# Scores ahead of everything in TensorE's written-out order, denominators inverted on one row per head, and more exponentials on VectorE

## The chip, the cores and the metric

One core of one Trainium2 chip. Time is device time in microseconds (us); the kernel before has a median of 2510.38 us over three runs (2509.66 to 2510.57). TensorE (PE) multiplies matrices, with weight loads beside it (PEld); VectorE (DVE), ScalarE (ACT) and GpSimd (POOL) work elementwise; SyncE (SP) issues the DMA transfers.

## The reference

Two layers, and each is a linear attention with a softmax feature map (A) followed by an ordinary softmax attention (B), both behind a layer norm and with a residual. Sequence 2048, width 1024, 32 heads of 32, bfloat16.

```python
def _A_ref(x, wqkv, w_phi, wo):          # q, k, v: 32 heads of 32
    pq = jnp.einsum("bhsd,hdf->bhsf", q, w_phi)
    pk = jnp.einsum("bhsd,hdf->bhsf", k, w_phi)
    phi_q = jnp.concatenate([_softmax(pq, axis=-1), _softmax(-pq, axis=-1)], axis=-1)
    phi_k = jnp.concatenate([_softmax(pk, axis=-1), _softmax(-pk, axis=-1)], axis=-1)
    kv = jnp.einsum("bhsf,bhsd->bhfd", phi_k, v)
    z  = jnp.einsum("bhsf->bhf", phi_k)
    num = jnp.einsum("bhqf,bhfd->bhqd", phi_q, kv)
    den = jnp.einsum("bhqf,bhf->bhq", phi_q, z)[..., None] + 1e-6
    o = num / den                        # then transposed, times wo

def _B_ref(x, wqkv, wo):
    scores = jnp.einsum("bhqd,bhkd->bhqk", q, k) * (Dh ** -0.5)
    p = _softmax(scores, axis=-1)
    o = jnp.einsum("bhqk,bhkd->bhqd", p, v)   # then transposed, times wo

for _ in range(2):
    x = x + _A_ref(_layernorm(x, axis=-1), A_wqkv, A_w_phi, A_wo)
    x = x + _B_ref(_layernorm(x, axis=-1), B_wqkv, B_wo)
```

## The kernel before

**How the program comes about.** The kernel doesn't issue instructions as it goes. It describes every piece of work as an `Op` with an engine, an assumed duration, dependencies, buffers and a priority (a due time; lower is earlier), and `Sched.run` plays these through a small model of the chip. The order in which the model starts the pieces is the order in which the instructions are written to each engine's queue; on the chip each engine then works through its queue in order. On each engine the model takes the ready piece with the lowest priority whose buffers can be had; it looks past at most 60 that can't start, and at nothing more than `WINDOW` = 80 ahead of the earliest piece not yet started. Buffers have quotas by class (`QUOTA`): SBUF pieces come from one large tile called `arena`, so nearly everything in the profile is called `arena`; PSUM has eight banks. A wait that the chip needs because a piece of arena is used again follows from where the model put it.

**The stages.** The sequence is cut into four chunks of 512 tokens, the heads into eight groups of four (`g`). Attention A is done chunk by chunk. Attention B has 32 turns a layer: a turn is one chunk of queries (`qc`) and one group of heads. The first 16 turns go over the groups for chunks 0 and 1, the rest over the groups for chunk 2 and then 3. A turn has two halves (`pp`), each with eight blocks of keys times four heads, so 64 units of 128 keys by 512 queries.

**Scores and exponentials.** Three units make a group. Their three matmuls (line 1006, each on 32 of TensorE's rows, beside one another) fill three banks of PSUM, banks 0 to 2 and 3 to 5 in turn; one ScalarE instruction (line 1012) takes the exponential of all 1536 columns into a tile of class `E`, of which there are five. The product with the values (line 1042) adds up in bank 6, with the sums of the exponentials (a matmul with ones) beside it: per half, two heads' outputs on 64 partitions and their denominators on the other 64, each denominator repeated on 32 partitions. A copy (line 1057, tile class `T`) empties bank 6 on VectorE. The priorities are the turn's due time less 2 for scores, less 3 for exponentials, less 1 for the products and less 4 for the copy.

**The filling.** Bank 7 belongs to everything else that TensorE does meanwhile: projections of the next heads' keys, queries and values, the output projection of finished chunks, and in the first layer the next layer's attention A on chunks 0 to 2, all through the helper at line 425 with priorities of their own. Where the model finds TensorE idle for a good part of 3.4 us, it writes idle matmuls (line 1253, with a weight of zeros).

**Units on VectorE.** `exp_dve` computes the exponential of two units at a time with ten VectorE instructions (lines 949 to 966) from bank 7. `EXTRA` says in which turns of which layer, and how many; these units are left out of ScalarE's groups.

**Denominators.** After the second half of a turn two transfers (lines 1083 and 1085, 128 KB each, on SP) bring both halves' denominators into one tile (`den`), four reciprocals of 128 columns (line 1087) invert it, and two products (line 1091) give the turn's output (`oT`), which the output projection reads later. The last turn of a layer goes another way, without transfers (lines 1067 to 1078).

Of the kernel before, what the change touches and what calls it, by code (L numbers as in the profile page):

```python
# [11 lines left out]
ALU = mybir.AluOpType  # L12
AX = mybir.AxisListType
BF16 = mybir.dt.bfloat16
F32 = mybir.dt.float32
# [5 lines left out]
C512 = 512  # L21
# [11 lines left out]


class Op:
    __slots__ = ("eng", "dur", "lat", "fn", "bufs", "prio", "mode", "ndep", "out", "t", "start", "seq", "accum")

    def __init__(self, eng, dur, lat, fn, bufs, prio, mode, seq):
        self.eng, self.dur, self.lat, self.fn, self.bufs = eng, dur, lat, fn, bufs
        self.prio, self.mode, self.seq = prio, mode, seq  # L40
        self.ndep, self.out, self.t, self.start, self.accum = 0, [], 0.0, None, None


LAT = {"PE": 0.25, "ACT": 0.2, "DVE": 0.1, "POOL": 0.2, "SP": 2.0, "AQ": 2.0}
# [3 lines left out]
class Sched:  # L48
# [11 lines left out]
    def op(self, eng, dur, fn, deps=(), bufs=(), prio=0.0, lat=None, mode=None):  # L60
        o = Op(eng, dur, LAT[eng] if lat is None else lat, fn, tuple(bufs), prio, mode, len(self.ops))
        for d in deps:
            if d is not None:
                d.out.append(o)
                o.ndep += 1
        for b in o.bufs:
            b.left += 1
        self.ops.append(o)
        return o
# [75 lines left out]
    def run(self):  # L145
        engines = list(LAT)
# [19 lines left out]
        started = {}  # L166
        for o in self.ops:
            if o.ndep == 0:
                heapq.heappush(ready[o.eng], (o.prio, o.seq, o))
        t, left, order = 0.0, len(self.ops), []  # L170
        while left:
            moved = False
            for e in engines:
                if busy[e] > t + 1e-9 or not ready[e]:
                    continue
                skipped = []
                pick = None
                while ready[e] and len(skipped) < 60:
                    item = heapq.heappop(ready[e])
                    if item[0] <= todo[front] + WINDOW and self._alloc(item[2].bufs):  # L180
                        pick = item[2]
                        break
                    skipped.append(item)
                for s in skipped:
                    heapq.heappush(ready[e], s)
                if pick is None and e == "PE" and self.idle is not None and self.live.get("S", 0):

                    recent = [r for r in recent if r[1] > t - SPELL]
                    worked = sum(r[1] - max(r[0], t - SPELL) for r in recent)
                    if worked >= KEEP * SPELL:  # L190
                        pass
                    elif self.bank_used[7]:

                        if accum:
                            pick = Op("PE", MM, LAT["PE"], self.idle_acc, (), 0.0, "c", 0)
                            left += 1
                    elif not self.live.get("fil", 0):
                        pick = Op("PE", MM, LAT["PE"], self.idle, (Buf("ps", 0, "idle", [(7,)]),), 0.0, "c", 0)
                        pick.bufs[0].left = 1
                        self.queue["idle"] = [list(pick.bufs), 0]  # L200
                        assert self._alloc(pick.bufs)
                        left += 1
                if pick is None:
                    continue
                if e == "PE":
                    recent.append((t, t + pick.dur))
                    if pick.accum is not None:
                        accum = pick.accum
                d = pick.dur
                if pick.mode is not None:  # L210
                    if mode[e] is not None and mode[e] != pick.mode:
                        d += SWITCH
                    mode[e] = pick.mode
                pick.start = t
                if pick.fn not in (self.idle, self.idle_acc):
                    started[pick.prio] = started.get(pick.prio, 0) + 1
                while front < len(todo) - 1 and started.get(todo[front], 0):
                    started[todo[front]] -= 1
                    front += 1
                busy[e] = t + d  # L220
                order.append(pick)
                left -= 1
                moved = True
                n += 1
                heapq.heappush(events, (t + d, n, pick, True))
                n += 1
                heapq.heappush(events, (t + d + pick.lat, n, pick, False))
            if moved:
                continue
            if not events:  # L230
                stuck = [(o.prio, o.eng, [(b.cls, b.at) for b in o.bufs]) for e in engines for _, _, o in ready[e]][:8]
                raise AssertionError(f"nothing can start at {t:.1f}: {left} left, {stuck}, live {self.live}")
            t = events[0][0]
            while events and events[0][0] <= t + 1e-9:
                _, _, o, own = heapq.heappop(events)
                if not own:
                    for b in o.bufs:
                        b.left -= 1
                        if b.left == 0:
                            self._release(b)  # L240
                for x in o.out:

                    if own != (x.eng == o.eng and x.eng not in ("SP", "AQ")):
                        continue
                    x.ndep -= 1
                    if x.ndep == 0:
                        heapq.heappush(ready[x.eng], (x.prio, x.seq, x))
        self.end = t
        return order

# [4 lines left out]
LONG = {"kT", "v", "slab", "slabk", "xn", "xn1", "kvacc", "kvm", "zm", "wnat"}  # L255
MODEST = {"slabk", "xn1", "e1", "vp1", "pkf", "lnw1", "w2o"}
QUOTA = {"pk": 3, "pv": 2, "kv": 1, "ln": 2, "mm": 2, "cmp": 2, "bc": 4, "num": 1, "wt": 4, "fil": 2,
# [4 lines left out]
SPELL = 3.4  # L262
KEEP = 0.75
# [3 lines left out]
POW2_0 = 0.998010015430466  # L267
POW2_C = (-2.753493604392706, 3.611980637904819, -2.738565741928622)
LEAD = 5.0
EXTRA = (lambda i: [(i % 2, 2)] if 12 <= i < 17 else [],  # L270
         lambda i: [(0, 2), (1, 2)] if 16 < i < 30 and i % 4 else [(i % 2, 2)] if 8 <= i < 30 else [])


def act_us(n):
    return n / 1200 + 0.064


def dve_us(n):
    return n / 960 + 0.15
# [6 lines left out]
def kernel(  # L286
# [15 lines left out]
    G = PO  # L302
# [67 lines left out]
    wdq_v = wd_q[:].rearrange("(po pi) f -> pi po f", pi=P)  # L370
    wdk_v = wd_k[:].rearrange("(po pi) f -> pi po f", pi=P)

    qd = dram_p.tile([P, 2 * G * C512], BF16, tag="qd")
    qd_v = qd[:].rearrange("p (c g n) -> p c g n", c=2, g=G)
    xd = dram_p.tile([P, 3 * PO * C512], BF16, tag="xd")
# [39 lines left out]
    def dma(prio, fn, deps=(), bufs=(), q="SP", kb=256, issue=0.55):  # L415
        return op(q, issue, fn, deps, bufs, prio, lat=2.0 + kb / 200.0)
# [554 lines left out]
    def attention(base, kT, vT, q_of, gate, extra):  # L971
# [16 lines left out]
        while i < len(units):  # L988
# [14 lines left out]
            def sfn(grp=grp, s_v=s_v):  # L1003
                for x, (qc, g, pp, d, j) in enumerate(grp):
# [4 lines left out]
                        rhs=q_of[(qc, g)][1]()[r, (pp + j // 2) % 2, :],  # L1009
                        start=True, stop=True, tile_position=(32 * j, 0))  # L1010
            so = op("PE", 0.24, sfn, deps + (gate if n == 0 else []), [s_b, *bufs], prio - 2, mode="r")
            ex = op("ACT", act_us(w * C512), lambda s_v=s_v, e_v=e_v, w=w: nc.scalar.activation(  # L1012
                out=e_v()[:, 0:w * C512], in_=s_v(), func=ACT.Exp, scale=4 * math.log(2)),
                [so], [s_b, e_b], prio - 3)
# [6 lines left out]
        if True:  # L1021
            for qc, g in turns:
# [41 lines left out]
                if end:  # L1064
# [15 lines left out]
                        [ln], [o_b, l_b, a_b], prio))  # L1080
                    oTs[qc][g] = (o_b, o_v, s)
                    continue
                m1 = dma(prio, lambda d_v=d_v, T=T: nc.sync.dma_start(out=d_v()[hi_, :], in_=T[0][1]()[hi_, :]),
                         [T[0][2]], [d_b, T[0][0]], kb=128)
                m2 = dma(prio, lambda d_v=d_v, T=T: nc.sync.dma_start(out=d_v()[lo_, :], in_=T[1][1]()[lo_, :]),
                         [T[1][2]], [d_b, T[1][0]], kb=128)
                rc = [op("DVE", 128 * 8 / 960 + 0.12, lambda b=b, d_v=d_v, r_v=r_v: nc.vector.reciprocal(  # L1087
                    out=r_v()[:, b * P:(b + 1) * P], in_=d_v()[:, b * P:(b + 1) * P]), [m1, m2], [d_b], prio)
                    for b in range(4)]
                o_b, o_v = sb("oT", C512)  # L1090
                s = [op("DVE", dve_us(512), lambda a=a, b=b, k=k, o_v=o_v, r_v=r_v, T=T: nc.vector.tensor_tensor(
                    out=o_v()[a, :], in0=T[k][1]()[a, :], in1=r_v()[b, :], op=ALU.mult),
                    rc, [o_b, r_b, T[k][0]], prio)
                    for k, (a, b) in enumerate(((lo_, hi_), (hi_, lo_)))]
                oTs[qc][g] = (o_b, o_v, s)
        return oTs, so

# [191 lines left out]
```

## Time and profile before

| | |
|---|---|
| median of three runs | 2510.38 us |
| the profiled execution | 2511.27 us, its span 2509.5 us |
| mean granted TensorE clock | 0.994 |
| exponentials (line 1012) of the first layer | first starts at 357.6 us, last ends at 1343.8 us |
| of the second layer | 1566.4 to 2497.5 us |
| their busy time | 1812.4 us in 1342 instructions |
| VectorE units | 37 of two blocks (lines 949 to 966), 9.0 us each |
| reciprocals (line 1087) | 248, 212.9 us busy |

The span runs from the first to the last instruction of the program. Busy times of an engine are shares of that span; instructions of one engine can overlap by some hundred ns, so the distance between two starts is shorter than the duration in a row.

### The profile page before, as it was taken

How to read it: one execution, taken by the hardware profiler on the slowest of the kernel's cores; microseconds unless marked ns; L12 is line 12 of the kernel's file. 1: busy time of each engine (PE TensorE's matmuls, PEld its weight loads, DVE VectorE, ACT ScalarE, POOL GpSimd, SP SyncE). 2: the span in 40 equal slices, each digit the busy share in tenths (PEclk: the TensorE clock that was granted, in tenths of full speed). 3: DMA queues.
4: the chain of work that ended last, by engine and by line, in shares of the span. 5: the costliest groups of instructions: out<-in, count | busy, mean ns of one | idle time of the engine just before them, and what ended most of it. 6: DMA issues, size and time to landing. Idle time of an engine off the chain costs nothing.

```text
span 2509.5 us, 62924 instructions
## 1 busy us (share of the span) xinstructions
PE 2368.6 (94%) x27872; PEld 893.4 (36%) x27872; DVE 1468.5 (59%) x2003; ACT 2145.4 (85%) x1897; POOL 26.1 (1%) x72
## 2 busy tenths in 40 slices
PE   7999999999999999999999999999999999999998
PEld 4443433333333333333333444333333333333333
DVE  6997653333356345654646766333356578687854
ACT  6335558999999999999996465699999999999998
POOL 0000000000000000000000000000000000000000
PEclk9999999999999999999999999999999999999999
DMA  9110012111121222222323001111121100110000
GB/s 219 33 44 1 22 21 48 35 36 44 41 62 42 56 54 69 77 66 69 114 65 116 1 5 38 36 36 35 40 62 27 35 27 27 29 33 27 25 25 27
DMA packets 185282, 117.39 MB, mean 47 GB/s; under 512 B 103344, under 2 KB 175024, under 8 KB 184240
## 3 DMA queue, kind: packets, MB, share of 16 engines
q1 hardware_dynamic: 183952, 111.26, 16.7%
q8 instruction: 218, 3.57, 0.6%
q10 hardware_dynamic: 1056, 2.10, 0.3%
q14 instruction: 56, 0.46, 0.1%
HBM read 62.46 MB, written 15.73 MB: 31 GB/s over the span
## 4 chain that ended last, share of the span: by engine, by line
ACT 46%; PE 31%; issue 12%; DVE 8%; SPq 1%; DMA 1%; ACTq 0%; DVEq 0%
ACT arena L1012 43%; PE psum L421 14%; PE psum L425 5%; PE psum L1042 5%; PE psum L1006 4%; DVE arena L616 1%; SPq L456 1%; PE psum L1253 1%; PE psum L780 1%; ACT arena L612 1%; DVE arena L625 1%; DVE arena L963 1%; DVE arena L662 1%; DVE arena L510 1%; DVE arena L514 1%
## 5 line engine op out<-in xcount | busy, mean ns | idle before, releaser
L1012 ACT ACTIVATE arena<-psum 128x1536 bf16<-128x1536 f32 x1342 | 1812.4, 1566 | 50.5 <-PE psum L1006 43.7
L1042 PE MATMUL psum<-arena 128*32 128x512 bf16 x4096 | 699.0, 385 | 11.6 <-ACT arena L1012 8.4
L1042 PE MATMUL psum<-arena,ones_bf 128*32 128x512 bf16 x4096 | 700.3, 386 | 0.0
L1006 PE MATMUL psum<-arena 32*128 32x512 bf16 x4022 | 522.8, 383 | 74.6 <-ACT arena L1012 68.3
L425 PE MATMUL psum<-arena 128*32 128x512 bf16 x8256 | 576.3, 380 | 4.9 <-DVE arena L625 1.3
L421 PE MATMUL psum<-arena 128*128 128x512 bf16 x2032 | 474.2, 383 | 18.1 <-DVE arena L514 5.4
L1006 PEld LDWEIGHTS <-arena 32*128 32x128 bf16 x4022 | 163.4, 91 | 574.8 <-issue 564.9
L421 PEld LDWEIGHTS <-arena 128*128 128x128 bf16 x2032 | 193.6, 98 | 265.8 <-issue 47.6
L425 PEld LDWEIGHTS <-arena 128*32 128x32 bf16 x8256 | 212.3, 96 | 209.8 <-issue 53.9
L1042 PEld LDWEIGHTS <-arena 128*32 128x32 bf16 x4096 | 165.8, 94 | 271.6 <-issue 246.5
L1087 DVE RECIPROCAL arena<-arena 128x128 f32<-128x128 f32 x248 | 212.9, 913 | 44.7 <-DMA arena<-arena 44.4
L1253 PE MATMUL psum<-xT,zero 128*32 128x512 bf16 x2712 | 218.5, 382 | 0.0
L839 DVE CAST arena<-psum 128x512 bf16<-128x512 f32 x112 | 77.3, 690 | 238.5 <-PE psum L425 238.1
L1042 PEld LDWEIGHTS <-ones_bf 128*32 128x32 bf16 x4096 | 158.4, 94 | 62.7 <-issue 50.8
L1057 DVE COPY arena<-psum 128x512 f32<-128x512 f32 x126 | 86.8, 689 | 157.3 <-PE psum L1042 155.6
L963 DVE SCALAR_TENSOR_TENSOR arena<-arena 128x1024 f32<-128x1024 f32 x111 | 135.6, 1222 | 2.3
L612 ACT ACTIVATE arena<-psum 128x512 bf16<-128x512 f32 x80 | 42.8, 600 | 86.1 <-PE psum L421 57.8
L742 ACT ACTIVATE arena<-psum 128x512 bf16<-128x512 f32 x128 | 69.8, 597 | 41.5 <-PE psum L421 32.0
L625 DVE TENSOR_TENSOR arena<-psum,arena 128x1024 bf16<-128x1024 f32 x64 | 78.3, 1224 | 39.6 <-PE psum L425 35.5
L510 DVE TENSOR_TENSOR arena<-xT,arena 128x1024 f32<-128x1024 bf16 x64 | 77.9, 1219 | 35.2 <-ACT arena L499 34.8
L1253 PEld LDWEIGHTS <-zero 128*32 128x32 bf16 x2712 | 70.3, 97 | 64.5 <-issue 16.8
L514 DVE TENSOR_TENSOR arena<-arena 128x1024 bf16<-128x1024 f32 x64 | 77.4, 1223 | 23.9 <-ACT arena L504 22.6
(100 smaller groups left out, 1428.3 us busy)
## 6 DMA issues: line engine op xcount, KB each, us to landing
arena<-arena SPq DMA_DIRECT2D x124, 128.0 KB, 2.2
arena<-in_A_wqkv_dram SPq DMA_DIRECT2D x10, 1024.0 KB, 5.5
arena<-in_B_wqkv_dram SPq DMA_DIRECT2D x32, 256.0 KB, 3.1
arena<-arena SPq DMA_DIRECT2D x256, 32.0 KB, 1.9
arena<-in_B_wo_dram SPq DMA_DIRECT2D x32, 256.0 KB, 3.0
arena<-wd_k SPq DMA_DIRECT2D x8, 1024.0 KB, 5.7
arena<-in_A_wo_dram SPq DMA_DIRECT2D x4, 1024.0 KB, 7.1
arena<-in_B_wqkv_dram SPq DMA_DIRECT2D x4, 1024.0 KB, 5.4
```

The lines of the kernel that those rows point to most:

```text
L421: nc.tensor.matmul(out_, lhsT=lhsT, rhs=rhs, start=start, stop=stop, skip_group_check=True)
L425: nc.tensor.matmul(out_[ks, :], lhsT=lhsT[:, ks], rhs=rhs, start=start, stop=stop, tile_position=(0, 32 * k), skip_group_check=True)
L510: s1 = op("DVE", dve_us(1024), lambda pr=pr, w_v=w_v: nc.vector.tensor_tensor(out=w_v(), in0=xT[:, pr, csl(c)], in1=m_v().unsqueeze(1).to_ ...
L514: fin.append(op("DVE", dve_us(1024), lambda pr=pr, w_v=w_v: nc.vector.tensor_tensor(out=xv()[:, pr, :], in0=w_v(), in1=r_v().unsqueeze(1). ...
L625: ml = op("DVE", dve_us(1024), lambda vpv=vpv, wv_=wv_, sv=sv: nc.vector.tensor_tensor(out=wv_()[:, :, :, 0:DH], in0=vpv().rearrange("p (h ...
L963: last = [op("DVE", dve_us(1024), lambda i=i, c=c: nc.vector.scalar_tensor_tensor(out=x_v(), in0=(x_v() if i else g_v()), scalar=c, in1=g_ ...
L1006: nc.tensor.matmul(out=s_v()[:, x * C512:(x + 1) * C512], lhsT=kT[g][1]()[r, pp, d * P:(d + 1) * P], rhs=q_of[(qc, g)][1]()[r, (pp + j // ...
L1012: ex = op("ACT", act_us(w * C512), lambda s_v=s_v, e_v=e_v, w=w: nc.scalar.activation(out=e_v()[:, 0:w * C512], in_=s_v(), func=ACT.Exp, s ...
L1042: nc.tensor.matmul(out=a_v()[col:col + 32, :], lhsT=v_v()[:, kc % 4, o:o + DH] if what == 0 else ones_bf[:], rhs=ev()[:, x * C512:(x + 1) ...
L1057: cp = op("DVE", dve_us(512), lambda t_v=t_v, a_v=a_v: nc.vector.tensor_copy(out=t_v(), in_=a_v()), [last], [a_b, t_b], prio - 4)
L1087: rc = [op("DVE", 128 * 8 / 960 + 0.12, lambda b=b, d_v=d_v, r_v=r_v: nc.vector.reciprocal(out=r_v()[:, b * P:(b + 1) * P], in_=d_v()[:, b ...
L1253: nc.tensor.matmul(psum[32 * k:32 * k + 32, 6 * C512:7 * C512], lhsT=zero[:], rhs=xT[:, 0, 0:C512], start=False, stop=False, tile_position ...
```

## The change

Three things change together.

Pieces of work get a flag `first`, set on all score groups from the third on; the model takes flagged pieces ahead of all others, whatever their priority. It looks past 400 pieces that can't start, not 60. There are six tiles of class `E`, not five.

Denominators are no longer inverted on 32 equal rows per head. Two transfers take one row per head (two from each half) and lay its 512 values out as 32 partitions of 16 (tile `cden`, 128 partitions by 16 columns). One reciprocal inverts them, a third transfer writes them to a tensor in HBM (`rd`), and a fourth reads them back with each row repeated on 32 partitions. The two products follow. The last turn's way is unchanged.

`EXTRA` gives VectorE two units (of two blocks) instead of one in turns 12 to 16 of the first layer; in the second, still one in turns 8 to 15, and in turns 16 to 29 two, or three in every third turn. In all 50 where there were 37, which is 26 blocks more.

```diff
-        self.ndep, self.out, self.t, self.start, self.accum = 0, [], 0.0, None, None
+        self.ndep, self.out, self.t, self.start, self.accum, self.first = 0, [], 0.0, None, None, False
...
-                heapq.heappush(ready[o.eng], (o.prio, o.seq, o))
+                heapq.heappush(ready[o.eng], (not o.first, o.prio, o.seq, o))
...
-                while ready[e] and len(skipped) < 60:
+                while ready[e] and len(skipped) < 400:
                     item = heapq.heappop(ready[e])
-                    if item[0] <= todo[front] + WINDOW and self._alloc(item[2].bufs):
-                        pick = item[2]
+                    if item[1] <= todo[front] + WINDOW and self._alloc(item[3].bufs):
+                        pick = item[3]
...
-                        heapq.heappush(ready[x.eng], (x.prio, x.seq, x))
+                        heapq.heappush(ready[x.eng], (not x.first, x.prio, x.seq, x))
...
-         "e": 6, "vp": 6, "e1": 4, "vp1": 4, "E": 5, "q2": 3, "kt": 3, "w2": 8, "w2o": 3, "oT": 26, "T": 4, "den": 2,
+         "e": 6, "vp": 6, "e1": 4, "vp1": 4, "E": 6, "q2": 3, "kt": 3, "w2": 8, "w2o": 3, "oT": 26, "T": 4, "den": 2,
...
-         "rs": 8, "pkf": 1, "part": 8, "w2r": 1,
+         "rs": 8, "pkf": 1, "cden": 2, "part": 8, "w2r": 1,
...
-EXTRA = (lambda i: [(i % 2, 2)] if 12 <= i < 17 else [],
-         lambda i: [(0, 2), (1, 2)] if 16 < i < 30 and i % 4 else [(i % 2, 2)] if 8 <= i < 30 else [])
+EXTRA = (lambda i: [(0, 2), (1, 2)] if 12 <= i < 17 else [],
+         lambda i: ([(0, 2), (1, 2)] if i % 3 else [(0, 2), (0, 5), (1, 4)]) if 16 <= i < 30 else [(i % 2, 2)] if 8 <= i < 16 else [])
...
+    rd = dram_p.tile([2 * NC * G * 4, C512], F32, tag="rd")
+    rd_v = rd[:].rearrange("(t h) n -> t h n", h=4)
+    gone = []
...
             so = op("PE", 0.24, sfn, deps + (gate if n == 0 else []), [s_b, *bufs], prio - 2, mode="r")
+
+            so.first = n >= 2
...
-                m1 = dma(prio, lambda d_v=d_v, T=T: nc.sync.dma_start(out=d_v()[hi_, :], in_=T[0][1]()[hi_, :]),
-                         [T[0][2]], [d_b, T[0][0]], kb=128)
-                m2 = dma(prio, lambda d_v=d_v, T=T: nc.sync.dma_start(out=d_v()[lo_, :], in_=T[1][1]()[lo_, :]),
-                         [T[1][2]], [d_b, T[1][0]], kb=128)
-                rc = [op("DVE", 128 * 8 / 960 + 0.12, lambda b=b, d_v=d_v, r_v=r_v: nc.vector.reciprocal(
-                    out=r_v()[:, b * P:(b + 1) * P], in_=d_v()[:, b * P:(b + 1) * P]), [m1, m2], [d_b], prio)
-                    for b in range(4)]
+                c_b, c_v = sb("cden", 16, dt=F32)
+                at_d = rd_v[len(gone)]
+                gone.append((qc, g))
+                m = [dma(prio, lambda k=k, c_v=c_v, T=T: nc.sync.dma_start(
+                    out=c_v()[64 * k:64 * k + 64, :],
+                    in_=T[k][1]()[64 * (1 - k):64 * (1 - k) + 64:32, :].rearrange("r (s c) -> r s c", c=16)),
+                    [T[k][2]], [c_b, T[k][0]], kb=4) for k in range(2)]
+                rc = op("DVE", 0.27, lambda c_v=c_v: nc.vector.reciprocal(out=c_v(), in_=c_v()), m, [c_b], prio)
+                aw = dma(prio, lambda c_v=c_v, at_d=at_d: nc.sync.dma_start(
+                    out=at_d.rearrange("h (s c) -> (h s) c", c=16), in_=c_v()), [rc], [c_b], kb=8)
+                bk = dma(prio, lambda r_v=r_v, at_d=at_d: nc.sync.dma_start(
+                    out=r_v(), in_=at_d.unsqueeze(1).to_broadcast([4, 32, C512])), [aw], [d_b], kb=256)
                 o_b, o_v = sb("oT", C512)
-                s = [op("DVE", dve_us(512), lambda a=a, b=b, k=k, o_v=o_v, r_v=r_v, T=T: nc.vector.tensor_tensor(
-                    out=o_v()[a, :], in0=T[k][1]()[a, :], in1=r_v()[b, :], op=ALU.mult),
-                    rc, [o_b, r_b, T[k][0]], prio)
-                    for k, (a, b) in enumerate(((lo_, hi_), (hi_, lo_)))]
+                s = [op("DVE", dve_us(512), lambda a=a, k=k, o_v=o_v, r_v=r_v, T=T: nc.vector.tensor_tensor(
+                    out=o_v()[a, :], in0=T[k][1]()[a, :], in1=r_v()[a, :], op=ALU.mult),
+                    [bk], [o_b, r_b, T[k][0]], prio)
+                    for k, a in enumerate((lo_, hi_))]
```

More of the change, by code (lines that the diff above doesn't have):

```diff
@@ L35 @@
 class Op:
-    __slots__ = ("eng", "dur", "lat", "fn", "bufs", "prio", "mode", "ndep", "out", "t", "start", "seq", "accum")
+    __slots__ = ("eng", "dur", "lat", "fn", "bufs", "prio", "mode", "ndep", "out", "t", "start", "seq", "accum", "first")
     def __init__(self, eng, dur, lat, fn, bufs, prio, mode, seq):
@@ L230, in run @@
             if not events:
-                stuck = [(o.prio, o.eng, [(b.cls, b.at) for b in o.bufs]) for e in engines for _, _, o in ready[e]][:8]
+                stuck = [(o.prio, o.eng, [(b.cls, b.at) for b in o.bufs]) for e in engines for _, _, _, o in ready[e]][:8]
                 raise AssertionError(f"nothing can start at {t:.1f}: {left} left, {stuck}, live {self.live}")
```

## The prediction

> **What bounds the kernel now.** I read the page first (busy time, the 40 slices, the costliest groups), then the windows, then ScalarE's and TensorE's rows in order of time, then the waits, last the transfers. In the slices the two attention stages are where ACT shows 9: slices 8 to 21 and 27 to 40.
>
> ```profile
> span 2509.5 us, 62924 instructions
> PE 2368.6 (94%) x27872; PEld 893.4 (36%) x27872; DVE 1468.5 (59%) x2003; ACT 2145.4 (85%) x1897; POOL 26.1 (1%) x72
> ...
> PE   7999999999999999999999999999999999999998
> ...
> DVE  6997653333356345654646766333356578687854
> ACT  6335558999999999999996465699999999999998
> ...
> L1012 ACT ACTIVATE arena<-psum 128x1536 bf16<-128x1536 f32 x1342 | 1812.4, 1566 | 50.5 <-PE psum L1006 43.7
> ...
> L1253 PE MATMUL psum<-xT,zero 128*32 128x512 bf16 x2712 | 218.5, 382 | 0.0
> ...
> L1087 DVE RECIPROCAL arena<-arena 128x128 f32<-128x128 f32 x248 | 212.9, 913 | 44.7 <-DMA arena<-arena 44.4
> ```
>
> TensorE's 94% is not a bound: L1253 is filling that multiplies zeros where nothing else is due. ScalarE in the windows is:
>
> ```profile
> 800.00:900.00 100.00, 96.09 (x1330) 33.17 (x1326) 38.70 (x50) 100.00 (x75) 0.00 (x0) 1.00 0.22 50
> 1000.00:1100.00 100.00, 92.47 (x1319) 36.67 (x1316) 63.19 (x92) 96.33 (x84) 2.90 (x8) 1.00 0.24 75
> 2300.00:2400.00 100.00, 91.66 (x1262) 31.24 (x1255) 85.27 (x103) 99.96 (x76) 0.00 (x0) 1.00 0.10 27
> ```
>
> Its cadence stands in its timeline: 44 exponentials in 59.36 us, less 1.57 for the last's own length: 1.34 us from start to start; over all neighbouring pairs the median is 1.331 us (a row's 1.566 us overlaps its neighbours). The first row is the longest wait at a stage's start.
>
> ```profile
> 368.44 1.45 ACT L1012 ACTIVATE arena<-psum 128x1536 bf16<-128x1536 f32 x1 [9.39 <-PE psum L1006]
> ...
> 1271.86 59.36 ACT L1012 ACTIVATE arena<-psum 128x1536 bf16<-128x1536 f32 x44
> ```
>
> The exponentials run from 357.6 to 1343.8 and from 1566.4 to 2497.5. Stage 1: 986.2 us = 680 x 1.331 (905.1) + 37.8 of other ScalarE work + 43.3 lost. Stage 2: 931.1 = 662 x 1.331 (881.1) + 8.6 + 41.4. About half of each loss (21.5 and 21.2) lies before the 26th exponential, where the last token chunk's keys are still being made; some 7 in each are slips of tens of ns. The rest, about 15 and 13, are waits, most of them for scores (L1006) that stand behind other TensorE work:
>
> ```profile
> PE psum L1006 <- ACT arena L1012: 68.3, 229, 3.7
> ...
> DVE arena L1087 <- DMA arena<-arena: 44.4, 28, 3.5
> ACT arena L1012 <- PE psum L1006: 43.7, 34, 9.4
> ```
>
> TensorE's prices, by starts in its timeline: from the scores' start to the next kind's 0.32 us, from the start of two groups of four column-tiled matmuls (x8) to the scores 0.55. So a group of four, or of three scores, is 0.21 us, and a turn between the kinds 0.11.
>
> ```profile
> 396.32 0.61 PE L425 MATMUL psum<-arena 128*32 128x512 bf16 x8
> 396.87 0.39 PE L1006 MATMUL psum<-arena 32*128 32x512 bf16 x3
> 397.19 1.48 PE L425 MATMUL psum<-arena 128*32 128x512 bf16 x24
> ```
>
> **The change part by part.** The sum is made against the profiled execution's own 2511.27 us (span 2509.5 and 1.8 around it), 0.9 above the median 2510.38.
>
> *More VectorE units.* A unit takes two 512-wide blocks off ScalarE. Units go from 5 to 10 in stage 1 and from 32 to 40 in stage 2, so 26 blocks leave; exponentials of three go from 680 to 676 and from 662 to 656 in the built programs. Ten fewer on a saturated engine: 10 x 1.331 = **-13.3 us**.
>
> *Scores first.* Both programs' TensorE orders can be counted. With the prices above I summed the work between each score group and the next, from the 21st group of each stage. Stretches over 1.9 us: 44 and 9 before, 18 and 2 after. What exceeds the 1.331 us cadence: 110 us before, 59 after. Two score tiles are in PSUM, so a stretch hurts only where its lateness outlasts the tile in hand; of the 28 us of waits one of 4 us, at 1856, is for a transfer, and order does not cure it. With the 53 long stretches 33 go, so 24 x 33/53 = **-15 us** (by the excess, 24 x 51/110 = -11); ends 0 and -28. At the start of a stage, work before the first score is the same instruction for instruction; then two more score groups get ahead of the block for the last chunk (8 groups instead of 6). Two exponentials are 2.7 us, and the stretch from the 9th to the 26th takes 21 us of TensorE work where it took 24; but the chunk's keys end the wait either way. **-3 us each, -6 in all**; ends 0 and -10.
>
> What falls due later: the delayed projections. Per 20 groups (26.6 us of ScalarE) the real TensorE work is 27.4, then 23.5 to 24.9 for the next eight such stretches: less than ScalarE's time in sum, so keys and queries still come in time. Between the stages the ScalarE order is identical and TensorE's work is 203.6 us for 203.4; at the end 16 more column matmuls follow the last scores, **+1 us**.
>
> *Denominators.* Per turn and not on the path: 4 reciprocals (248 x 0.913 = 226 us of VectorE) become 62 of 16 columns; the nearest row, 32 columns, takes 0.353, so at most 22 us. The two transfers of 128 KB (2.2 us to land) become four: two of 4 KB, one of 8 KB to HBM, one of 256 KB back. SP issues 124 more at about 0.6 us, 74 us on a queue that mostly waits. The chain to the product grows, by rows, from 2.2 + 3.4 to between 1.9 + 0.4 + 1.7 + 2.1 and, with 8.1 (the slowest row) for both ends, 18 us. Its reader is the output projection, a stage later except for the last turns, whose final one keeps the old direct path; the source tiles come round again two turns (52 us) later. So **0** off the path. What it can hold up is VectorE, which waits in order at the reciprocal and at the product, and SP, which waits for the reciprocal with the next queries and keys behind it.
>
> *VectorE's room.* A unit costs 2 x 0.690 + 2 x 0.687 + 2 x 0.693 + 3 x 1.222 + 1.225 = 9.0 us: 13 x 9.0 = 117 us more against 204 less. The tight place is turns 16 to 28 of stage 2: busy 78 + 74 + 80 + 85 = 318 of 400 us there (windows from 2000 to 2400), 282 in the turns' 355; plus 8 units (72), less the reciprocals (44), gives 311 us in some 342 of ScalarE, 91%, leaving 2.4 us a turn. Sixteen PE matmuls more for the units' scores have room. In the new order 5.5 us of work on average stand between the second copy and the reciprocal and 8.5 before the product, against 2 and 4 us of transfers by the middle rows; a few will come late. **+3 us**; ends 0 (the work covers them) and +25 (next part).
>
> Sum: -13.3 - 15 - 6 + 1 + 3 = -30: 2511.3 - 30 = 2481, or **2480** beside the median.
>
> Against the change speaks a rule of the Trainium skill, "DMA: Bandwidth & Descriptors", section "Rules for kernel authors": an outermost dimension of size c under 16, such as a leading broadcast, confines a transfer to c engines. The 256 KB return has 4 outermost, the two gathers 2. With that page's 27 GiB/s per engine and 2 us fixed, an estimate from its figures alone is some 4.3 us for the return, and the sum stays as it is. No row of before has such a shape; the 256 KB loads with 128 outermost land in 3.1 us.
>
> **The rivals.**
> *The waits only move* (0.17). Late projections stall the scores as often as early ones did. For it: TensorE has only some 5 to 10% of room in the first nine stretches of each stage; against it the counts above. Then only the units pay: 2511.3 - 13.3 + 1 + 3 = 2502 at worst, 2495 with the start's gain.
> *The transfers come late and VectorE becomes the bound* (0.08). At 8.1 us for gather and return, a turn waits 8.1 - 5.5 at the reciprocal and about 1.7 + 8.1 - 8.5 at the product, 3.9 us. Room is 2.4, so 1.5 x 13 = 20 us come back, and 25 with some in stage 1: about 2503. The page above says the same of the cause.
> *Slower: TensorE's own queue* (0.08). A score put at the instant its tile comes free makes TensorE wait for ScalarE, with projections behind it. Place: groups 20 to 180 of each stage, with 16 us of room for 160 groups, 0.1 us per group. Before, it waited 68.3 us over 1342 groups, 0.05 each. Each 0.1 us more than the room costs 16 us a stage, 32 in all; the gain is gone at 0.2 us a group. At 0.25, 2511.3 - 30 + 48 = 2529. Against it: a TensorE that is late does not wait at scores, so the waits shrink as it becomes the bound.
> *Nearly all waits go* (0.09): -13.3 - 28 - 10 = 2460.
> That the order does not put scores first is excluded by the counts.
>
> **How the numbers follow.** The forecast, 2465 to 2495, has 0.58. The range 2460 to 2505 leaves out the slower rival and the tails. No change is within 0.2%, 5 us, which is about what a measurement can tell: faster 0.58 + 0.17 + 0.09 + 0.05 = 0.89, same 0.03, slower 0.08.
>
> **What would show it.** ScalarE's group falls from 1342 to 1332 with the same 1.331 us cadence; its wait for the score matmuls (now another line) falls from 43.7 to about 28, most of it the two starts; idle matmuls fall from 2712 to 2048; the reciprocal group is 62 at under 0.353 us. Stage lengths: about 972 and 915 us. Wrong if VectorE is 95% busy at 2000 to 2400 with waits on the return transfer, or if scores wait for key or query transfers.

## The result and the profile after

The changed kernel takes 2854.94 us (median of 4 runs, 2851.68 to 2858.06) where the kernel before takes 2510.02: 1.1374 times as long, 95% interval 1.1355 to 1.1394. The forecast was 2480, with a range of 2460 to 2505. The profiled execution has a span of 2851.6 us, 342.1 more than before.

The page of the changed kernel:

```profile
span 2851.6 us, 61282 instructions
...
PE 2448.5 (86%) x26898; PEld 882.0 (31%) x26964; DVE 1382.5 (48%) x1947; ACT 2162.0 (76%) x1887; POOL 24.9 (1%) x72
...
ACT  5345568888778888878785555888789787888887
...
L1017 ACT ACTIVATE arena<-psum 128x1536 bf16<-128x1536 f32 x1332 | 1827.3, 1472 | 381.2 <-DMA arena<-arena 263.6
```

The exponentials are the 1332 that were counted. But ScalarE, saturated before, shows mostly 7 and 8 in both attention stages: its idle time before line 1017 has gone from 50.5 to 381.2 us, and the releaser named is a transfer within the arena. Stage 1 lasts 1164.9 us (986.2 before), stage 2 1094.0 (931.1). These 341.6 us are the whole difference. The waits of the changed kernel:

```profile
PE psum L1009 <- ACT arena L1017: 300.5, 310, 7.5
...
ACT arena L1017 <- DMA arena<-arena: 263.6, 120, 9.0
...
DVE arena L1102 <- DMA arena<-rd: 72.6, 25, 7.5
DVE arena L842 <- DMA arena<-arena: 71.0, 22, 9.8
DVE arena L1096 <- DMA arena<-arena: 68.6, 27, 7.3
ACT arena L1017 <- PE psum L1009: 68.1, 85, 9.4
...
ACT arena L1017 <- PE psum L1047: 36.1, 54, 1.6
```

120 waits of an exponential for a transfer, 2.2 us each; the gathers of denominators (line 1092) are 124. Rows of the changed kernel in order of time, SP and ScalarE, show one of them:

```profile
605.60 1.45 ACT L1017 ACTIVATE arena<-psum 128x1536 bf16<-128x1536 f32 x1
...
607.07 0.56 SPq L1092 DMA_DIRECT2D arena<-arena  x1
...
608.99 4.14 ACT L1017 ACTIVATE arena<-psum 128x1536 bf16<-128x1536 f32 x3 [1.94 <-DMA arena<-arena]
```

The gather is issued 0.02 us after an exponential ends (605.60 + 1.45 = 607.05), and the next exponential starts 1.92 us after that issue; the gather's median time to landing is 1.82 us. It stands between two exponentials like a barrier, though it reads copies of bank 6 and writes a small tile of its own class, and the exponential writes a tile of class E.

The built program says the same. For each wait of an exponential for one of the denominators' first transfers I counted the exponentials issued in between, in the program's order:

```
kernel before     102 waits for its 124 transfers   median 16.5 exponentials later   none at the next
changed kernel    124 waits for its 124 gathers     median 0                         120 at the very next
```

In the kernel before such a wait comes when a tile's memory is used again, long after the transfer has landed. In the changed kernel it has nothing to do with memory used again. The barrier has two sides: 121 of the 124 gathers themselves wait for an exponential, 109 of them for the last one written before them. In the kernel before 29 of the 124 transfers wait for an exponential, none for the last one.

### The profile page after: what moved, and what is told of

Same layout as the page of the kernel before. It is cut to its first block, busy times and chain, and to the rows that moved or that the text cites. A ratio compares the mean times of both kernels' runs of the same rounds, so it can differ in the third digit from the quotient of the medians.

```text
span 2851.6 us, 61282 instructions
## 1 busy us (share of the span) xinstructions
PE 2448.5 (86%) x26898; PEld 882.0 (31%) x26964; DVE 1382.5 (48%) x1947; ACT 2162.0 (76%) x1887; POOL 24.9 (1%) x72
## 3 DMA queue, kind: packets, MB, share of 16 engines
q1 hardware_dynamic: 199328, 112.28, 14.4%
## 4 chain that ended last, share of the span: by engine, by line
PE 35%; ACT 30%; DMA 12%; issue 11%; DVE 10%; SPq 2%; ACTq 0%; another core or an unknown queue 0%; DVEq 0%
ACT arena L1017 28%; PE psum L424 12%; DMA arena<-arena 8%; PE psum L1047 7%; PE psum L428 6%; PE psum L1009 6%; PE psum L1264 2%; DMA arena<-rd 2%; DVE arena L966 1%; DVE arena L619 1%; DMA arena<-in_A_wqkv_dram 1%; SPq L459 1%; DVE arena L628 1%; PE psum L783 1%; DMA arena<-in_B_wo_dram 1%
## 5 line engine op out<-in xcount | busy, mean ns | idle before, releaser
L1017 ACT ACTIVATE arena<-psum 128x1536 bf16<-128x1536 f32 x1332 | 1827.3, 1472 | 381.2 <-DMA arena<-arena 263.6
L1009 PE MATMUL psum<-arena 32*128 32x512 bf16 x3996 | 559.2, 408 | 306.7 <-ACT arena L1017 300.5
L1047 PE MATMUL psum<-arena 128*32 128x512 bf16 x4096 | 706.0, 413 | 12.3 <-DVE arena L1062 8.4
L428 PE MATMUL psum<-arena 128*32 128x512 bf16 x8256 | 611.7, 400 | 20.6 <-DVE arena L842 9.1
L424 PE MATMUL psum<-arena 128*128 128x512 bf16 x1973 | 466.8, 382 | 20.2 <-DVE arena L1083 4.1
L1009 PEld LDWEIGHTS <-arena 32*128 32x128 bf16 x3996 | 172.6, 92 | 875.9 <-issue 861.8
L966 DVE SCALAR_TENSOR_TENSOR arena<-arena 128x1024 f32<-128x1024 f32 x150 | 183.3, 1222 | 17.2 <-PE psum L1047 10.5
L1264 PE MATMUL psum<-xT,zero 128*32 128x512 bf16 x2048 | 187.5, 427 | 0.0
L1102 DVE TENSOR_TENSOR arena<-arena 64x512 bf16<-64x512 f32 x124 | 84.9, 685 | 114.6 <-DMA arena<-rd 72.6
L952 DVE TENSOR_SCALAR arena<-psum 128x512 f32<-128x512 f32 x100 | 68.9, 689 | 131.6 <-PE psum L947 104.8
L619 DVE TENSOR_REDUCE arena<-arena 128x32 f32<-128x1024 bf16 x64 | 77.7, 1214 | 51.8 <-ACT arena L615 46.4
```

The lines of the kernel that those rows point to most:

```text
L424: nc.tensor.matmul(out_, lhsT=lhsT, rhs=rhs, start=start, stop=stop, skip_group_check=True)
L428: nc.tensor.matmul(out_[ks, :], lhsT=lhsT[:, ks], rhs=rhs, start=start, stop=stop, tile_position=(0, 32 * k), skip_group_check=True)
L619: red = op("DVE", dve_us(1024), lambda ev=ev, sv=sv: nc.vector.reduce_sum(out=sv(), in_=ev().rearrange("p s (h d) -> p (s h) d", d=DH), ax ...
L966: last = [op("DVE", dve_us(1024), lambda i=i, c=c: nc.vector.scalar_tensor_tensor(out=x_v(), in0=(x_v() if i else g_v()), scalar=c, in1=g_ ...
L1009: nc.tensor.matmul(out=s_v()[:, x * C512:(x + 1) * C512], lhsT=kT[g][1]()[r, pp, d * P:(d + 1) * P], rhs=q_of[(qc, g)][1]()[r, (pp + j // ...
L1047: nc.tensor.matmul(out=a_v()[col:col + 32, :], lhsT=v_v()[:, kc % 4, o:o + DH] if what == 0 else ones_bf[:], rhs=ev()[:, x * C512:(x + 1) ...
```

## The experiments

Three theories at first. A: the gather reads two rows 32 partitions apart (`:32` in its source), and such a step is taken as touching the whole of the arena, in which everything lies; so whatever writes to the arena next waits for it (a false conflict). B: the transfers are slow, in 64-byte pieces, on few engines and through HBM. C: scores first starves the projections.

**The copies of bank 6 in a tile of their own**

```diff
-SBUF_ARENA = 174 * 1024
+SBUF_ARENA = 166 * 1024
...
+    town = const.tile([P, 4 * C512], F32, tag="town")
...
-                    t_b, t_v = sb("T", C512, dt=F32)
+                    t_b, _ = sb("T", 16, dt=F32)
+                    t_v = lambda s=len(tcount) % 4: town[:, s * C512:(s + 1) * C512]
+                    tcount.append(0)
```

> Edit: the changed kernel, but the copies of bank 6 (class T) go to an SBUF tile of their own (8 KB a partition; the arena shrinks from 174 to 166 KB). The gather keeps its shape: two rows, 32 partitions apart, in 64-byte pieces. Theory A (a false conflict: a read that steps over partitions counts as touching the whole of the tile that it reads from, so the next exponential, which writes to the same tile arena, waits until the gather has landed, 2 us for each of 124): ScalarE's 264 us of waits on transfers go, 2854.9 falls to 2465 to 2500. Theory B (the transfers themselves are slow: 64-byte pieces, few engines, HBM there and back, VectorE held): the transfers are the same, so it stays at 2800 or more. Theory C (scores first starves the projections): stays at 2800 or more.

2503.75 us, 0.9982 of the kernel before (0.9973 to 0.9991), 351 us below the changed kernel. The gather is the same transfer, shape and pieces included, and in the trace no exponential waits for a transfer; the largest wait left is the one for scores:

```profile
L1019 ACT ACTIVATE arena<-psum 128x1536 bf16<-128x1536 f32 x1332 | 1803.7, 1619 | 60.8 <-PE psum L1011 43.6
```

B falls as the cause of the 345 us, and so does C.

**Gathers of one row**

```diff
-                    in_=T[k][1]()[64 * (1 - k):64 * (1 - k) + 64:32, :].rearrange("r (s c) -> r s c", c=16)),
-                    [T[k][2]], [c_b, T[k][0]], kb=4) for k in range(2)]
+                    in_=T[k][1]()[64 * (1 - k) + 32 * r:64 * (1 - k) + 32 * r + 1, :].rearrange("r (s c) -> r s c", c=16)),
+                    [T[k][2]], [c_b, T[k][0]], kb=2) for k in range(2) for r in range(2)]
```

(the destination is split alike.)

> Edit: the changed kernel, but each gather of two rows 32 partitions apart becomes two gathers of one row each (248 transfers of 2 KB for 124 of 4 KB); the source stays in the arena. Theory A: a row of one partition conflicts with nothing else, so 2465 to 2500, or a few us over the kernel with T in its own tile for the SP queue's 124 further issues. Theory B: more and smaller transfers, 2850 to 2950. Theory C: as the changed kernel, 2855.

2505.69 us, 0.9989 (0.9978 to 1.0000). Twice the transfers, source in the arena, and the time is gone too. Both are 4 to 6 us above the upper end that A gave; what keeps them there is the question of the second set.

**The old denominators under the new order**

```diff
-                m = [dma(prio, lambda k=k, c_v=c_v, T=T: nc.sync.dma_start(
...
+                m1 = dma(prio, lambda d_v=d_v, T=T: nc.sync.dma_start(out=d_v()[hi_, :], in_=T[0][1]()[hi_, :]),
+                         [T[0][2]], [d_b, T[0][0]], kb=128)
...
+                rc = [op("DVE", 128 * 8 / 960 + 0.12, lambda b=b, d_v=d_v, r_v=r_v: nc.vector.reciprocal(
...
```

> Edit: the changed kernel with the denominators of the kernel before (two transfers of 128 KB, four reciprocals of 128 columns); scores first and the 26 blocks stay. Theories A and B: 2470 to 2500, VectorE now over 95% busy in turns 16 to 28 of the second stage since the 3.4 us of reciprocals a turn are back, so some 5 to 20 us above the kernel with one-row gathers. Theory C: 2800 or more.

The two transfers of 128 KB, the four reciprocals and the products are those of the kernel before. 2497.61 us, 0.9953 (0.9936 to 0.9970). Scores first doesn't starve anything: stage 1 falls to 967.2 us. Stage 2 takes 938.8, where with scores first and without the 26 blocks it takes 916.4 (see below). VectorE's load is the likely reason; this kernel's windows show it (after the stretch and its length, busy us of PE, PEld, DVE, ACT and POOL with their instructions, the granted clock, the DMA share and GB/s):

```profile
2000.00:2200.00 200.00, 183.33 (x2516) 64.12 (x2515) 171.21 (x207) 188.61 (x140) 0.00 (x0) 0.98 0.10 27
2200.00:2400.00 200.00, 182.34 (x2525) 65.29 (x2518) 186.12 (x223) 182.87 (x136) 0.00 (x0) 1.00 0.09 25
```

VectorE (third figure) is at 171 and then 186 of 200 us, which is 86 and 93%, under the 95 expected; ScalarE (fourth) falls to 183. The time was expected to lie above that of the kernel with one-row gathers and lies 8 us below it: that kernel has a loss of its own, which comes further down.

**The new denominators alone, on the kernel before**

Against the kernel before:

```diff
-                m1 = dma(prio, lambda d_v=d_v, T=T: nc.sync.dma_start(out=d_v()[hi_, :], in_=T[0][1]()[hi_, :]),
...
+                m = [dma(prio, lambda k=k, c_v=c_v, T=T: nc.sync.dma_start(
...
+                rc = op("DVE", 0.27, lambda c_v=c_v: nc.vector.reciprocal(out=c_v(), in_=c_v()), m, [c_b], prio)
```

> Edit: the kernel before with only the new denominators. Theory A: 2510 plus 124 waits of about 2.1 us on ScalarE and what follows from them, 2780 to 2850. Theory B: the same sign, but with VectorE's idle time before the reciprocal and the products as the larger part. Theory C: 2500 to 2520.

2897.66 us in one run, beyond the upper end. Its waits hold the same row at the same size:

```profile
ACT arena L1015 <- DMA arena<-arena: 263.5, 114, 10.0
```

So the denominators alone make the whole loss, and the other two parts took some 40 us off it.

**Neighbouring partitions**

Each head's denominator stands on 32 equal rows, so rows 31 and 32 hold the same two heads as rows 0 and 32.

```diff
-                    in_=T[k][1]()[64 * (1 - k):64 * (1 - k) + 64:32, :].rearrange("r (s c) -> r s c", c=16)),
+                    in_=T[k][1]()[64 * (1 - k) + 31:64 * (1 - k) + 33, :].rearrange("r (s c) -> r s c", c=16)),
```

> Edit: the changed kernel, and the gather takes partitions 31 and 32 of its 64, which are neighbours (each head's denominator stands on 32 partitions, so the values are the same), in place of 0 and 32. Number, size and pieces of the transfers stay. If the step of 32 partitions makes the false conflict, the waits are gone and the return is as late as ever: 2498 to 2508, as with one-row gathers. If any gather of two rows conflicts: 2855.

2511.17 us, 1.0008 (0.9996 to 1.0019), 3 us above the range, 344 us below the changed kernel. Not any gather of two rows conflicts: the step of 32 partitions does. How much of the arena such a gather is taken to touch, the runs don't show. In the built program the waits that remain come a median of 15.5 exponentials later, none at the next one, and no gather waits for the last exponential before it.

**What holds the mended kernels at 2504 to 2511**

Their own loss is in this row, of the kernel with neighbouring partitions and, second, of that with one-row gathers:

```profile
DVE arena L1102 <- DMA arena<-rd: 119.1, 41, 8.2
```

```profile
L1102 DVE TENSOR_TENSOR arena<-arena 64x512 bf16<-64x512 f32 x124 | 85.0, 685 | 128.3 <-DMA arena<-rd 122.1
```

VectorE waits in order at the product for the return, with the emptying of banks 6 and 7 behind it. From issue to landing the return takes a median of 5.1 us in the traces of the changed and the mended kernels, where loads of the same 256 KB take 3.0 to 3.3. It sends 5 updates of its semaphore after its issue where those send 16. The planner allowed 3.83 us.

First the planner's number alone, on the kernel with one-row gathers:

```diff
-                    out=r_v(), in_=at_d.unsqueeze(1).to_broadcast([4, 32, C512])), [aw], [d_b], kb=256)
+                    out=r_v(), in_=at_d.unsqueeze(1).to_broadcast([4, 32, C512])), [aw], [d_b], kb=520)
```

> Edit: the kernel with one-row gathers, and the planner is told that the return takes what the trace of it shows (5.1 us from issue to landing; it assumed 0.55 + 3.28 = 3.83), so that the products stand later in VectorE's order. No instruction is added or taken away. Theory D (the rest of the forecast's gain, 2505.7 where 2480 was forecast, is lost where VectorE waits in order at a product for a return that comes 1.3 us later than planned, 122 us in 46 waits, with the emptying of banks 6 and 7 behind it): those waits fall below 50 us and the time to 2480 to 2495. Theory E (the waits at the products cost nothing, and the remaining losses are projections that come late since scores go first): 2500 to 2510.

2487.25 us, 0.9909 (0.9894 to 0.9924): 18 us from putting the products later. The wait falls from 122.1 to 65.1 us, not under 50:

```profile
DVE arena L1102 <- DMA arena<-rd: 65.1, 24, 8.3
```

Then the return itself, again on the kernel with one-row gathers:

```diff
-                bk = dma(prio, lambda r_v=r_v, at_d=at_d: nc.sync.dma_start(
-                    out=r_v(), in_=at_d.unsqueeze(1).to_broadcast([4, 32, C512])), [aw], [d_b], kb=256)
+                bk = [dma(prio, lambda h=h, r_v=r_v, at_d=at_d: nc.sync.dma_start(
+                    out=r_v()[32 * h:32 * h + 32, :], in_=at_d[h:h + 1, :].to_broadcast([32, C512])), [aw], [d_b], kb=64)
+                    for h in range(4)]
```

> Edit: the kernel with one-row gathers, and the return as four transfers of 64 KB, one per head, each with 32 rows outermost, in place of one of 256 KB with 4 outermost. Rule of four engines (in the traces a return sends 5 updates of its semaphore where others send 16): each lands in 1.9 to 2.5 us like the 64 KB rows, the last some 1.8 us of issuing later, so about 4 us in place of 5.1; with the planner's own allowance for four issues the products wait little. Theory D: 2480 to 2498. Theory E: 2500 to 2512, by three more issues a turn.

2472.10 us, 0.9848 (0.9832 to 0.9864), below the range. Each of the four lands in 2.1 us with 16 updates; the wait at the products is 37.3 us. The edit changes the planner's allowance along with the shape, so the 33.6 us against one-row gathers are for both. Its waits, page and windows:

```profile
DVE arena L1103 <- DMA arena<-rd: 37.3, 26, 6.3
```

```profile
span 2472.9 us, 61880 instructions
...
L1017 ACT ACTIVATE arena<-psum 128x1536 bf16<-128x1536 f32 x1332 | 1798.6, 1675 | 30.8 <-PE psum L1009 26.6
```

```profile
2000.00:2200.00 200.00, 183.77 (x2532) 63.66 (x2529) 160.68 (x201) 200.00 (x150) 0.00 (x0) 1.00 0.11 31
2200.00:2400.00 200.00, 181.47 (x2435) 62.62 (x2436) 175.11 (x215) 199.43 (x149) 0.00 (x0) 0.99 0.10 27
```

Stage 1 is 967.7 us and stage 2 910.3; the forecast's 972 and 915. ScalarE is saturated again, with VectorE at 84% beside it.

The same return beside the tile for the copies of bank 6:

```diff
+    town = const.tile([P, 4 * C512], F32, tag="town")
...
+                bk = [dma(prio, lambda h=h, r_v=r_v, at_d=at_d: nc.sync.dma_start(
```

> Edit: the changed kernel with the copies of bank 6 in an SBUF tile of their own (the gather again one of two rows, 32 partitions apart, two a turn) and the return in four. If the gather's shape costs nothing once its source is a tile of its own, as the kernel with one-row gathers (2472) or a little less for 124 fewer issues: 2466 to 2476. If the two-row gather is itself slow: 2485 or more.

2473.07 us, 0.9859 (0.9845 to 0.9874): the two-row gather costs nothing once its source is a tile of its own.

And beside the gather of neighbouring partitions:

```diff
+                    in_=T[k][1]()[64 * (1 - k) + 31:64 * (1 - k) + 33, :].rearrange("r (s c) -> r s c", c=16)),
...
+                bk = [dma(prio, lambda h=h, r_v=r_v, at_d=at_d: nc.sync.dma_start(
```

> Edit: as the kernel whose gather takes neighbouring partitions, and the return in four transfers of one head each. By the steps so far, 2855 less 350 for the conflict less 33 for the return: 2466 to 2475, the fastest with no further memory.

2472.10 us, 0.9853 (0.9839 to 0.9868). With the change of one index and the return in four, the changed kernel beats the kernel before by 36 us, with no further memory.

**The other two parts by themselves**

Against the kernel before, scores first (with the longer look and six tiles of class `E`):

```diff
-                heapq.heappush(ready[o.eng], (o.prio, o.seq, o))
+                heapq.heappush(ready[o.eng], (not o.first, o.prio, o.seq, o))
...
+            so.first = n >= 2
```

> Edit: the kernel before with scores first alone (the flag, the longer look, six tiles of class E); units and denominators as before. By the forecast's steps: -15 of waits, -6 at the two starts, +1 at the end: 2486 to 2494, gain in both stages alike. Theory E: no gain, 2505 to 2515.

2481.61 us, 0.9891 (0.9876 to 0.9905): 27 us gained and 4 below the range; in the profiled executions 14.4 in stage 1 and 14.7 in stage 2. ScalarE's idle time before its exponentials:

```profile
L1013 ACT ACTIVATE arena<-psum 128x1536 bf16<-128x1536 f32 x1342 | 1810.9, 1676 | 32.4 <-PE psum L1006 24.8
...
ACT arena L1013 <- PE psum L1006: 24.8, 7, 9.4
```

Seven waits are left of 34, the longest, 9.4 us, at a stage's start: more of the steady ones went than the count of long stretches gave.

Against the kernel before, the units:

```diff
-EXTRA = (lambda i: [(i % 2, 2)] if 12 <= i < 17 else [],
-         lambda i: [(0, 2), (1, 2)] if 16 < i < 30 and i % 4 else [(i % 2, 2)] if 8 <= i < 30 else [])
+EXTRA = (lambda i: [(0, 2), (1, 2)] if 12 <= i < 17 else [],
+         lambda i: ([(0, 2), (1, 2)] if i % 3 else [(0, 2), (0, 5), (1, 4)]) if 16 <= i < 30 else [(i % 2, 2)] if 8 <= i < 16 else [])
```

> Edit: the kernel before with the 26 further blocks on VectorE alone. By the forecast: 10 exponentials fewer are 13.3 us, but the reciprocals' 3.4 us a turn are still there, so that VectorE has 25.2 + 3.2 us of work for 26.4 us in turns 16 to 28 of the second stage: the first stage 5 us shorter, the second 5 to 25 longer, 2505 to 2530 in all. If VectorE's load does not matter: 2497.

2526.67 us, 1.0071 (1.0056 to 1.0086). Stage 1 is 2.9 us shorter, stage 2 16.9 longer: the units cost more than they bring as long as the old reciprocals are there.

Against the kernel with one-row gathers and the return in four, the old units:

```diff
-EXTRA = (lambda i: [(0, 2), (1, 2)] if 12 <= i < 17 else [],
-         lambda i: ([(0, 2), (1, 2)] if i % 3 else [(0, 2), (0, 5), (1, 4)]) if 16 <= i < 30 else [(i % 2, 2)] if 8 <= i < 16 else [])
+EXTRA = (lambda i: [(i % 2, 2)] if 12 <= i < 17 else [],
+         lambda i: [(0, 2), (1, 2)] if 16 < i < 30 and i % 4 else [(i % 2, 2)] if 8 <= i < 30 else [])
```

> Edit: the kernel with one-row gathers and the return in four (2472.1), but the units of the kernel before (37 of two blocks). Theory F (with the waits gone, ScalarE is the bound and a saved exponential is worth its cadence): 10 x 1.331 = 13 us longer, 2483 to 2488. Theory G (VectorE's further 117 us hide the gain again): 2470 to 2476.

2482.18 us, 0.9893 (0.9876 to 0.9909), a little under Theory F's range, so with the reciprocals gone the 26 blocks bring 10.1 us.

## Why the prediction was wrong

The step that failed is the one on the denominators: "What it can hold up is VectorE, which waits in order at the reciprocal and at the product, and SP, which waits for the reciprocal with the next queries and keys behind it", and before it "**0** off the path". It followed the data: who reads the result, and when. It left out what else waits for the transfer. ScalarE, the engine on the path, was held at 120 of 124 gathers, 263.6 us. Both programs had been counted for the order of their instructions and not for their waits, where 120 of 124 stood to be read. Nor was it among the rivals: the one on the slow side named TensorE's queue, and the one on late transfers VectorE.

ScalarE's idle time before its exponentials grew by 330.7 us, nearly all of the 342. Beside the 263.6, its waits for scores grew from 43.7 to 68.1 us and those for the product with the values (line 1047) from 1.2 to 36.1. What made TensorE late there was not tested apart; the emptying of bank 7 (line 842) was held 71.0 us for the same transfers. The granted clock also fell, to 0.931, and comes back with the mended kernels (0.985 to 0.995); whether it added to the time is open.

The steps one by one, in kernels without the conflict:

- *More VectorE units*, -13.3: measured -10.1 beside the mended new denominators, and +18 on the kernel before. With scores first and the old denominators it is +16.0 (2497.61 against 2481.61), so it is the denominators that turn the sign. That the parts depend on one another was in the working (91% with the reciprocals gone) but not that the sign of the units hangs on it.
- *Scores first*, -15 and -6, with 1 at the end: -20 forecast, -27 measured alone. Right in kind, short by a third; the far ends were -28 and -10. By the traces the stages' starts, up to the 26th exponential, became 4.5 and 4.2 us shorter, and what follows 10.0 and 10.8.
- *VectorE's room*, +3: mis-sized. With the return as it was, it cost 33.6 us (2505.69 against 2472.10), beyond the end of 25; 18.4 of it came back with the planner's number alone. The rival of late transfers had this mechanism and, with both transfers at 8.1 us, 25 us; 5.1 us for the return was enough, since VectorE stands waiting with everything behind it, and the sum of its busy time says little of that.
- The rule cited, of the Trainium skill, "DMA: Bandwidth & Descriptors", section "Rules for kernel authors" (an outermost dimension of size c under 16 confines a transfer to at most c engines): the trace agrees. The return, with 4 outermost, sends one update of its semaphore 1.0 us after its issue and four between 4.4 and 5.1 us, where each of the four transfers with 32 outermost sends 16 and lands in 2.1 us. The prediction's estimate for the return was 4.3 us. The gathers with two outermost send 3 updates and land in 1.8 us all the same.
- *The waits only move* and *TensorE's own queue*: neither happened. With scores first alone TensorE's waits for ScalarE rose from 68.3 to 98.1 us, 0.07 per group, under the 0.1 of room, and the time fell.

The parts add up: -27.0 and -10.1 are -37, and with both mends the kernel takes 2472, 36.5 us off the kernel before. That this lies near the forecast of 2480 needs the return in four, which the forecast didn't have; with the conflict alone removed it is 2504 to 2511, at the end of the range or beyond it.

## What to carry to other kernels

Where one large tile holds everything, a conflict that is only in the bookkeeping can make any access a barrier: before a transfer is costed at nothing, read in the built program who waits for it, and how many instructions later. An access that steps over partitions is the first to look at; a neighbouring row or a tile of its own does the same work without it. And an estimated landing time that is written into an order is part of the program: 1.3 us too little on one transfer a turn cost 18 us.

## What was not expected of the hardware

A transfer of 256 KB whose source had 4 outermost took 5.1 us from issue to landing; as four of 64 KB with 32 outermost, each took 2.1. Gathers of 4 KB in 64-byte pieces took 1.8 us, no more than 32 KB transfers in 512-byte rows (1.9). In the changed kernel, where TensorE's scores wait 300.5 us for ScalarE (68.3 before), its granted clock was 0.83 in one window (2300 to 2400 us) and 0.93 over the span, where the kernel before has 1.00 and 0.99; that the waiting lowers the clock was not tested.
